# A hashed-attention and gated-MLP kernel: the last output row in three column parts, and one DMA transpose for three head pairs of the last batch

## The chip, the cores and the metric

The kernel runs on one core of one Trainium2 chip. The metric is the device time of one execution in microseconds (us). A core has five engines with a queue each: TensorE (PE; its weight loads are shown as PEld), VectorE (DVE), ScalarE (ACT), GpSimd (POOL) and SyncE (SP), which here only issues DMAs. The median of three runs is the time of a kernel; the profile is a further execution, recorded by the hardware.

## The reference

Four batches, eight heads, 768 positions, 64 columns a head. Queries and keys are hashed to six bits by the signs of a projection; a query attends to the keys with its own hash value only. The result, with heads side by side (3072 rows of 512), goes through a gated layer with a residual.

```python
q_bits = (np.einsum('bhsd,dk->bhsk', q, proj) > 0)          # k likewise; six bits are a bucket
mask = q_bucket[:, :, :, None] == k_bucket[:, :, None, :]
scores = np.where(mask, scale * q @ k.T, -1e9)
attn = softmax(scores);  x = (attn @ v), heads side by side   # 3072 x 512
ffn_out = (gelu(x @ w_gate) * (x @ w_val)) @ w_out            # 512 -> 1536 -> 512
return x + sigmoid(x @ w_res) * ffn_out
```

## The kernel before

**Stages.** The order of all work is written out by hand: each engine runs its instructions in the order in which the code issues them. Heads are taken in pairs, four pairs to a batch, 16 in all. A pair takes nine slots of the main loop (L612 on); in each slot TensorE computes scores for one chunk (`scores`, L380), ScalarE takes their exponential (L385) and TensorE multiplies older exponentials with the values (`values`, L354). At the end of a head, `finish` (L299) divides by the row sums on VectorE and writes the result to `x_tok[b]`, an array of 128 partitions by 4 pairs by 6 blocks by 128 columns, positions on partitions.

**Transposes of x.** The gated layer needs x with its columns on partitions, in `x_sb[b]`. For most pairs `finish` issues a DMA transpose of that pair's six 128x128 blocks on SP's queue (L310). The last pair of a batch goes another way where there is no time for a DMA: `x_turn` (L335) transposes it on TensorE, and ScalarE and VectorE copy it (L340, L341). In the last batch the pairs 0, 1 and 2 go by DMA and pair 3 by `x_turn`.

**The gated layer.** After the last slot of a batch `gv_mm` (L393) and `gate_val` (L403) compute gate and value for twelve blocks of 128 hidden columns, in buffers of the PSUM pool `sc_ps`: TensorE matmuls (L399), ScalarE's Gelu (L416), VectorE's product into `hh` (L419). In the last batch the two first `gv_mm` calls, for pairs 0 to 2, are issued right behind the last attention work (L639), ahead of `x_turn`. `project` (L425) then gives the output, six rows of blocks to a batch, 128 output rows each: four matmuls against `wr` (L431), ScalarE's Tanh (L435), twelve matmuls of `hh` against `wo` into `fps` (L445), two multiply-adds on VectorE (L448, L451), and a store on SP (L453). It is a generator; for batches 0 to 2 its matmuls are spread over the next batch's attention, for the last batch they run at the end, one block row after another. There `fps` lies in `sc_ps` (two buffers, in turn), otherwise in the bank "f" of `mm_ps`, which the last batch's output does not use.

**The last block row.** The very last one (batch 3, t = 5) is computed in two column parts of 384 and 128 columns, `(0, 3)` and `(3, 4)` in units of 128: twelve matmuls, two multiply-adds and a store for the first, then the same for the second.

**DMA lanes.** Each hardware DMA (those issued by SP or ACT, 113 in this kernel) reports its end on one of eight semaphores, here called lanes 0 to 7, taken in turn; SP waits for the lane's previous DMA before it issues a new one on it. At the end of the program, under the line number of the launch (L679), SP waits for everything: first for POOL's DMAs, then lane 0, 1, 2 and so on to lane 7, two semaphores an instruction, then for the engines, and then a barrier over all engines follows. 113 is 14 × 8 + 1, so the last store is on lane 0.

Of the kernel before, what the change touches and what calls it, by code (L numbers as in the profile page):

```python
# [17 lines left out]
def kernel(  # L18
# [12 lines left out]
    nc = tc.nc  # L31
    B, H, S, D = q.shape
# [4 lines left out]
    KM = DMODEL // P  # L37
    KF = DFF // P
    T = S // P
    HP = H // 2  # L40
# [32 lines left out]
    x_tok, x_sb = {}, {}  # L73
# [89 lines left out]
    for s in range(3):  # L163
        n = KF // 3
# [134 lines left out]
    def finish(p, hi):  # L299
        b, hp = divmod(p, HP)  # L300
        if hp == 0 and hi == 0:
            x_tok[b] = x_pool.tile([P, HP, T, 2 * D], BF16, tag="x_tok", name="x_tok")
            x_sb[b] = x_pool.tile([P, HP, T, P], BF16, tag="x_sb", name="x_sb")
        o = av.pop((p, hi))
        rec = sm_pool.tile([P, T], FP32, tag="rec", name="rec")
        nc.vector.reciprocal(rec, o[:, 0:T, D])
        nc.vector.tensor_mul(x_tok[b][:, hp, :, hi * D:(hi + 1) * D], o[:, 0:T, 0:D],
                             rec.unsqueeze(2).to_broadcast([P, T, D]))
        if hi == 1 and (0 < b < B - 1 or hp < HP - (2 if b == 0 else 1)):
            nc.sync.dma_start_transpose(out=x_sb[b][:, hp],  # L310
                                        in_=x_tok[b][:, hp].rearrange("p t n -> p (t n)"))

# [32 lines left out]
    def values(p, c, e):  # L345
        va = vaug[p]
        for i in range(2):
            hi, parts = banks[2 * c + i]
            first = p < HP and (p, hi) not in av
            opened(p, hi)  # L350
            off = i * 512
            for (jt, qt0, nq) in parts:
                for qt in range(qt0, qt0 + nq):
                    nc.tensor.matmul(av[p, hi][:, qt, :], e[:, off:off + P],  # L354
                                     va[:, hi, jt, 0:D + 1],
                                     start=first, stop=(p >= HP and jt == T - 1),
                                     skip_group_check=True)
                    first = False
                    off += P
            if (2 * c + i + 1) % NCH == 0:  # L360
                if p < HP:
                    preset(p, hi)
                if (p, hi) not in late:
                    finish(p, hi)
# [60 lines left out]
    def project(b):  # L425
        hh = hidden[b]
        for t in range(T):
            last = b == B - 1 and t == T - 1
            rps = mm_ps.tile([P, DMODEL], FP32, tag="r", name="rps")
            for kk in range(KM):  # L430
                nc.tensor.matmul(rps, x_sb[b][:, kk, t, :], wr[:, kk, :],  # L431
                                 start=(kk == 0), stop=(kk == KM - 1))
                if kk == KM - 1:
                    th = g_pool.tile([P, DMODEL], FP32, tag="th", name="th")
                    nc.scalar.activation(th, rps, AF.Tanh, scale=0.5)  # L435
                yield
            o = o_pool.tile([P, DMODEL], FP32, tag="o", name="o")
            for k0, k1 in ((0, 3), (3, 4)) if last else ((0, KM),):
                cs = slice(k0 * P, k1 * P)
                if b < B - 1:  # L440
                    fps = mm_ps.tile([P, DMODEL], FP32, tag="f", name="fps")
                else:
                    fps = sc_ps.tile([P, DMODEL], FP32, tag="sp", name="fps")
                for m in range(KF):
                    nc.tensor.matmul(fps[:, cs], hh[:, m, bass.ts(t, P)], wo[:, m, cs],  # L445
                                     start=(m == 0), stop=(m == KF - 1))
                    yield
                nc.vector.scalar_tensor_tensor(o[:, cs], th[:, cs], 1.0, fps[:, cs],  # L448
                                               op0=ALU.add, op1=ALU.mult)
                o3 = o[:, cs].rearrange("p (k n) -> p k n", n=P)  # L450
                nc.vector.scalar_tensor_tensor(o3, o3, 0.5, x_tok[b][:, k0:k1, t, :],  # L451
                                               op0=ALU.mult, op1=ALU.add)
                nc.sync.dma_start(out_t[b, t][:, cs], o[:, cs])  # L453
# [90 lines left out]
    hash_pe((1,), 4, (4,))  # L544
    turns_pe(1, (6, 6, 8, 9))
    at(6, lambda: finish(0, 0), lambda: tr(2, 1))
    at(8, lambda: tr(3, 0))
    at(9, lambda: tr(3, 1))
    at(11, lambda: finish(0, 1))
    at(5, lambda: vals_a(1))  # L550
    at(7, lambda: vals_s(1))
# [60 lines left out]
    for s in range(LAST):  # L612
        p, c = divmod(s, NCH)
        b, slot = divmod(s, NSLOT)
# [10 lines left out]
        if slot == NSLOT - 1:  # L625
            values(*pending.pop(0))
            ps = (HP * (b + 1), HP * (b + 1) + 1)
            if b == 0:
                nc.scalar.activation(table, warm[:, 0:1], AF.Gelu)
                begun = [gv_mm(0, 0, wg, 0, KM - 1)]  # L630
                values(*pending.pop(0))
                begun.append(gv_mm(0, 0, wv, 0, KM - 1))
                x_turn(b, HP - 1)
                hashed(ps, 0, 3)
                gate_val(b, begun, lambda: hashed(ps, 3, 4))
            else:
                mlp_mm(4)
                flush()
                begun = [gv_mm(b, 0, w, 0, KM - 1) for w in (wg, wv)]  # L639
                if b < B - 1:  # L640
                    mlp_mm(NMM)
                    hashed(ps, 0, 2)
                    gate_val(b, begun, lambda: hashed(ps, 2, 4))
                else:
                    x_turn(b, HP - 1)
                    mlp_mm(HELD - 7)
                    gv(b, 0, lambda: mlp_mm(NMM))
                    gate_val(b, begun, lambda: mlp_mm(3))
            done[0] = 0
            mlp.append(project(b))  # L650
# [33 lines left out]
```

## Time and profile before

| what | value |
|---|---|
| median of 3 runs | 347.27 us (346.83 to 347.31) |
| span of the profiled execution | 345.9 us (345.875) |
| TensorE matmul busy | 337.9 us, 98% of the span |
| weight loads busy | 204.4 us, 59% |
| VectorE, ScalarE, GpSimd busy | 191.5, 206.9, 86.1 us |
| granted TensorE clock | full in all 40 slices |
| DMA | 42.90 MB, mean 124 GB/s |
| chain that ended last | TensorE 89%, ScalarE 5%, VectorE 3%, issue 1%, DMA 1% |
| DMA transposes of x | 13, median 2.8 us from issue to landing |
| stores of a whole block row | 23 of 256 KB, median 2.0 us to landing |
| the last two stores | 192 KB and 64 KB, 1.9 and 1.6 us to landing |

The span is that of one recorded execution; the runs' times are measured from outside and lie some 1.4 us above it. Groups are named by line, engine and operation, and `out<-in` by the program's tiles. A chain of waits follows the work that ended last back in time, from each step to what released it. Where a text gives a start to three decimals, it is the start of that instruction in the trace; the views round to one or two.

### The profile page before, as it was taken

The numbers are of one execution on the slowest core, as the hardware profiler recorded it, in microseconds if no ns is written. First come the engines' busy times: TensorE is split into PE (matmuls) and PEld (weight loads), VectorE is DVE, ScalarE is ACT, GpSimd is POOL, SyncE is SP. The second block draws the span as 40 slices with busy tenths as digits, with TensorE's granted clock in tenths as the row PEclk, the third lists the DMA queues.
The fourth block names the chain that finished last, engine by engine and source line by source line (L and its number), as shares of the span: only waits on it lengthen the run. The fifth ranks groups of instructions, "written<-read, shape, count | busy, mean of one in ns | idle before, by whom it ended". The sixth has DMA issues, their size and how long they took to land.

```text
span 345.9 us, 7597 instructions
## 1 busy us (share of the span) xinstructions
PE 337.9 (98%) x3112; PEld 204.4 (59%) x3112; DVE 191.5 (55%) x403; ACT 206.9 (60%) x232; POOL 86.1 (25%) x162
## 2 busy tenths in 40 slices
PE   8999999999999999999999999999999999999994
PEld 5667665655666655555666665655566665556442
DVE  6877757755344856757344784747244444333333
ACT  3889973226999952225999882222999984223120
POOL 4779940343055000270044100242030000000000
PEclk9999999999999999999999999999999999999999
DMA  7939999979376843518366642725430220000022
GB/s 218 377 67 239 247 265 195 159 89 223 121 178 196 195 106 78 106 34 154 85 182 190 223 117 61 136 48 105 79 100 32 55 55 30 32 1 0 32 75 78
DMA packets 71171, 42.90 MB, mean 124 GB/s; under 512 B 49504, under 2 KB 68192, under 8 KB 71136
## 3 DMA queue, kind: packets, MB, share of 16 engines
q1 hardware_dynamic: 64720, 37.17, 42.4%
q0 software_dynamic: 6336, 5.24, 10.2%
q8 instruction: 24, 0.39, 0.4%
q14 instruction: 11, 0.09, 0.1%
q10 hardware_dynamic: 80, 0.00, 0.0%
HBM read 29.36 MB, written 6.29 MB: 103 GB/s over the span
## 4 chain that ended last, share of the span: by engine, by line
PE 89%; ACT 5%; DVE 3%; issue 1%; DMA 1%; SPq 0%; DVEq 0%; ACTq 0%
PE sp L399 36%; PE fps L445 18%; PE sp L380 15%; PE av L354 8%; PE rps L431 5%; ACT e L385 4%; PE hs L205 3%; PE pt L259 2%; DMA ld<-in_q_dram 1%; DVE o L451 1%; DVE o L448 1%; DVE nat L224 0%; PE hs L234 0%; DVE ht L215 0%; DVE hh L419 0%
## 5 line engine op out<-in xcount | busy, mean ns | idle before, releaser
L385 ACT ACTIVATE e<-sp 128x1024 bf16<-128x1024 f32 x144 | 143.8, 1027 | 13.4 <-PE sp L380 7.8
L416 ACT ACTIVATE gt<-sp 128x768 bf16<-128x768 f32 x48 | 38.9, 811 | 93.0 <-PE sp L399 93.0
L380 PE MATMUL sp<-aug,aug 71*128 71x256 bf16 (+1 forms) x384 | 86.1, 325 | 1.1 <-ACT e L385 0.6
L445 PE MATMUL fps<-wo,hh 128*128 128x512 bf16 (+2 forms) x300 | 79.5, 370 | 0.0
L419 DVE TENSOR_TENSOR hh<-gt,sp 128x768 bf16<-128x768 bf16 x48 | 45.8, 955 | 50.5 <-PE sp L399 45.3
L399 PE MATMUL sp<-x_sb,wg 128*128 128x512 bf16 (+1 forms) x384 | 71.0, 326 | 0.1
L399 PE MATMUL sp<-x_sb,wv 128*128 128x512 bf16 (+1 forms) x384 | 70.9, 326 | 0.2 <-DVE hh L419 0.2
L354 PEld LDWEIGHTS <-e 128*128 128x128 bf16 x1152 | 53.3, 97 | 29.1 <-issue 1.4
L354 PE MATMUL av<-va,e 128*128 128x65 bf16 x1152 | 58.9, 193 | 0.1
L399 PEld LDWEIGHTS <-wv 128*128 128x128 bf16 x384 | 37.5, 98 | 25.1 <-issue 0.4
L399 PEld LDWEIGHTS <-wg 128*128 128x128 bf16 x384 | 36.6, 98 | 26.3 <-issue 3.0
L445 PEld LDWEIGHTS <-hh 128*128 128x128 bf16 x300 | 27.5, 97 | 22.7 <-issue 0.3
L448 DVE SCALAR_TENSOR_TENSOR o<-th,fps 128x512 f32<-128x512 f32 (+2 forms) x25 | 16.6, 666 | 36.6 <-PE fps L445 32.0
L380 PEld LDWEIGHTS <-aug 71*128 71x128 bf16 x384 | 29.4, 97 | 10.9 <-issue 2.1
L184 POOL TENSOR_SCALAR nat<-ld 128x768 bf16<-128x768 f32 (+1 forms) x16 | 14.1, 884 | 76.8 <-DMA aug<-nat 73.0
L281 POOL TENSOR_TENSOR v<-ldv 128x384 f32<-128x384 f32 x16 | 16.0, 998 | 66.7 <-DMA ldv<-in_v_dram 66.6
L194 DVE STREAM_TRANSPOSE t<-ld 128x768 f32<-128x768 f32 (+1 forms) x34 | 30.8, 913 | 1.2 <-DMA ld<-in_q_dram 1.0
L333 DVE COPY av<-av 128x390 f32<-128x390 f32 x24 | 13.6, 567 | 30.0 <-PE av L329 30.0
L431 PE MATMUL rps<-wr,x_sb 128*128 128x512 bf16 x96 | 27.1, 378 | 0.0
L435 ACT ACTIVATE th<-rps 128x512 f32<-128x512 f32 x24 | 14.3, 594 | 18.4 <-PE rps L431 18.4
L224 DVE TENSOR_SCALAR nat<-htp 32x72 bf16<-32x72 f32 x96 | 21.9, 228 | 1.8
L451 DVE SCALAR_TENSOR_TENSOR o<-o,x_tok 128x512 f32<-128x512 f32 (+2 forms) x25 | 18.2, 727 | 0.9
(61 smaller groups left out, 191.2 us busy)
## 6 DMA issues: line engine op xcount, KB each, us to landing
ldv<-in_v_dram SPq DMA_DIRECT2D x16, 384.0 KB, 5.5
out_dram<-o SPq DMA_DIRECT2D x23, 256.0 KB, 2.0
ld<-in_q_dram SPq DMA_DIRECT2D x15, 384.0 KB, 5.2
ld<-in_k_dram SPq DMA_DIRECT2D x15, 384.0 KB, 6.2
wg<-in_moe_w_gate_dram POOLq DMA_DIRECT2D x4, 384.0 KB, 8.0
wv<-in_moe_w_val_dram POOLq DMA_DIRECT2D x4, 384.0 KB, 9.8
wo<-in_moe_w_out_dram POOLq DMA_DIRECT2D x3, 512.0 KB, 6.2
wr<-in_moe_w_res_dram POOLq DMA_DIRECT2D x1, 512.0 KB, 12.8
```

Of the source, the lines that this page charges most:

```text
L194: nc.vector.transpose(t32[p, side][:, sl].rearrange("p c h n -> p (c h n)"), raw[p, side][:, sl].rearrange("p c d -> p (c d)"))
L224: engs[a % len(engs)].tensor_scalar(nat_of(x)[32 * a:32 * a + 32, :, D:D + NBITS], ht[32 * j:32 * j + 32, :, NBITS * a:NBITS * (a + 1)], 0 ...
L354: nc.tensor.matmul(av[p, hi][:, qt, :], e[:, off:off + P], va[:, hi, jt, 0:D + 1], start=first, stop=(p >= HP and jt == T - 1), skip_group ...
L380: nc.tensor.matmul(sp[:, off:off + nq * P], ks[0:KA, hi * T + jt, :], qs[0:KA, hi * T + qt0:hi * T + qt0 + nq, :], start=True, stop=True)
L385: nc.scalar.activation(e, sp, AF.Exp, scale=float(ALPHA))
L399: nc.tensor.matmul(sp[:, c0:c1], w[:, kk, bass.ts(m, P)], xs[:, kk, c0:c1], start=(kk == 0), stop=(kk == KM - 1))
L416: nc.scalar.activation(gt, sp[:, 0:S], AF.Gelu)
L419: nc.vector.tensor_mul(hidden[b][:, m, :], gt, ps[1][:, 0:S])
L431: nc.tensor.matmul(rps, x_sb[b][:, kk, t, :], wr[:, kk, :], start=(kk == 0), stop=(kk == KM - 1))
L445: nc.tensor.matmul(fps[:, cs], hh[:, m, bass.ts(t, P)], wo[:, m, cs], start=(m == 0), stop=(m == KF - 1))
L448: nc.vector.scalar_tensor_tensor(o[:, cs], th[:, cs], 1.0, fps[:, cs], op0=ALU.add, op1=ALU.mult)
L451: nc.vector.scalar_tensor_tensor(o3, o3, 0.5, x_tok[b][:, k0:k1, t, :], op0=ALU.mult, op1=ALU.add)
```

## The change

Two edits. In `finish`, the pairs 0, 1 and 2 of the last batch are no longer transposed one by one as they are finished; when pair 2 is finished, a single DMA transpose of eighteen blocks is issued for all three. In `project`, the last block row is computed in three column parts, of 256, 128 and 128 columns. The first two take the two buffers of `sc_ps`, the third takes the bank "f" of `mm_ps`.

```diff
         nc.vector.tensor_mul(x_tok[b][:, hp, :, hi * D:(hi + 1) * D], o[:, 0:T, 0:D],
                              rec.unsqueeze(2).to_broadcast([P, T, D]))
-        if hi == 1 and (0 < b < B - 1 or hp < HP - (2 if b == 0 else 1)):
+        if hi == 1 and b == B - 1:
+            if hp == HP - 2:
+                nc.sync.dma_start_transpose(out=x_sb[b][:, 0:HP - 1].rearrange("p k t n -> p (k t) n"),
+                                            in_=x_tok[b][:, 0:HP - 1].rearrange("p k t n -> p (k t n)"))
+        elif hi == 1 and (b > 0 or hp < HP - 2):
             nc.sync.dma_start_transpose(out=x_sb[b][:, hp],
                                         in_=x_tok[b][:, hp].rearrange("p t n -> p (t n)"))
...
             o = o_pool.tile([P, DMODEL], FP32, tag="o", name="o")
-            for k0, k1 in ((0, 3), (3, 4)) if last else ((0, KM),):
+            for k0, k1 in ((0, 2), (2, 3), (3, 4)) if last else ((0, KM),):
                 cs = slice(k0 * P, k1 * P)
-                if b < B - 1:
+                if b < B - 1 or k0 == KM - 1:
                     fps = mm_ps.tile([P, DMODEL], FP32, tag="f", name="fps")
                 else:
                     fps = sc_ps.tile([P, DMODEL], FP32, tag="sp", name="fps")
```

Two transposes fewer and one store more make 112 hardware DMAs, 14 × 8, so that the last store is on lane 7. The order of the closing waits is the same. No other instruction changes its place on any engine; the first gate matmul of the last batch waits for one DMA where three matmuls waited for one each.

## The prediction

> **What bounds the kernel now.** I read the page's busy table first, then the chain of waits, then the records of the last eight microseconds, because all that the change does to the output lies there.
>
> ```profile
> PE 337.9 (98%) x3112; PEld 204.4 (59%) x3112; DVE 191.5 (55%) x403; ACT 206.9 (60%) x232; POOL 86.1 (25%) x162
> ```
>
> TensorE is busy for 98% of the span, at the full granted clock in every slice. What can be saved without taking work from it is the stretch in which it no longer runs: from its last matmul to the end. The chain of waits over that stretch (start, length, what):
>
> ```profile
> 337.99 0.86 PE rps L431 x4
> 338.85 1.96 PE fps L445 x12
> 340.81 0.04 DVEq L448
> ...
> 340.89 0.56 DVE o L448
> ...
> 341.48 0.56 DVE o L451
> 342.04 0.21 DVE o L448
> ...
> 342.27 0.29 DVE o L451
> ```
>
> The reader is to see that the twelve last 128-column matmuls are not in this chain. VectorE is still at the 384-column part when they end, and the 128-column part queues behind it. The timeline of the same stretch shows it from the other side; the second multiply-add of the last part starts only when the first part's has ended:
>
> ```profile
> 341.48 0.56 DVE L451 SCALAR_TENSOR_TENSOR o<-o,x_tok 128x384 f32<-128x384 f32 x1
> 341.96 0.28 DVE L448 SCALAR_TENSOR_TENSOR o<-th,fps 128x128 f32<-128x128 f32 x1
> 342.06 0.86 SPq L453 DMA_DIRECT2D out_dram<-o  x2
> 342.27 0.29 DVE L451 SCALAR_TENSOR_TENSOR o<-o,x_tok 128x128 f32<-128x128 f32 x1
> ```
>
> After that come a store and SP's closing waits. The view of what SP waited for, the issue table, and the view of the closing line in two stretches (344.1 to 344.6, then 344.6 to 345.2):
>
> ```profile
> SPq L679 <- DMA out_dram<-o: 1.1, 1, 1.1
> ...
> out_dram<-o SPq DMA_DIRECT2D x1, 64.0 KB, 1.6
> ...
> L679 SPq EVENT_SEMAPHORE  x5: 28/28/28, 344.2 to 344.5; - x5
> ...
> L679 SPq EVENT_SEMAPHORE  x3: 28/28/28, 344.8 to 345.0; - x3
> L679 SPq DRAIN  x2: 7/7/7, 345.0 to 345.1; - x2
> ```
>
> The store is issued at 342.589 and has landed at 344.142, 1.553 later. Then SP still works through eight waits, from 344.159 to 344.971, and reaches its first drain at 345.044. They are two per instruction, 0.06 to 0.09 apart, but for one pause of 0.38 between 344.453 and 344.833. All eight stand behind the landing because the last store is hardware DMA number 113 and so counts on lane 0, which is waited for first of the eight lanes. From landing to that drain 0.902 goes by; the rest of the end (to 345.875) is a barrier that the change does not touch.
>
> **The change, part by part.**
>
> *TensorE.* Twelve matmuls of 384 columns become twelve of 256 and twelve of 128; the last twelve of 128 stay. The pitch is 215 ns for 512 columns (four in 0.86) and 163 for 384 (twelve in 1.96), which is 0.41 ns a column and some 2.5 ns besides, so 109 for 256 and 56 for 128. The old 128-column run agrees: its last matmul starts 0.614 after its first, 56 each. Before: 12 × (163 + 56) = 2.63. After: 12 × (109 + 56 + 56) = 2.65. TensorE ends 0.03 later: the last matmul is done and signalled at 341.51 in place of 341.48.
>
> *VectorE.* From 553 and 279 ns for 384 and 128 columns (first multiply-add) a 256-column one takes 416; from 558 and 292 the second takes 425. Part one: its twelve matmuls start at 338.685, the last at 339.886, and with 272 for that one (between 219 and 326) it is signalled at 340.17. The wake-up took 0.08 before, so VectorE starts at 340.25, ends its second step at 341.13, and the store goes out at 341.15. Part two: 341.05 to 341.65 (the next instruction starts 0.08 before the last one ends, as above), store at 341.68. Part three: its matmuls are ready at 341.51 + 0.08 = 341.59, VectorE is free at 341.57. So 341.59 + 0.279 + 0.034 + 0.292 = 342.20, and the store is issued at 342.22. Before it was 342.589: **0.37 earlier**. There is no slack left on either side, 0.02 between the two engines.
>
> *Stores.* One more on SP: 0.332 of issue plus a lane wait, 0.43 in all between two issues. The three go out 0.53 apart, so it lies beside VectorE's work; were VectorE faster it would cost up to 0.43. The last store has the old last one's shape, so it lands 1.55 later, at 343.78. The two old stores were issued 0.52 apart and landed 0.2 apart, thus in parallel.
>
> *The lane.* Two DMAs fewer for x and one more store make 112, so the last store counts on lane 7, whose wait is the last of the eight. The other seven waits are met by landings that lie before 343.25 and run while the last store is under way: SP is free at 342.56, six of them and the pause end by 343.4, lane 6 follows. After 343.78 there remain one wait (0.017) and the step to the drain (0.073): 343.87 in place of 345.04. Of this 1.18 the lane gives 0.902 − 0.09 = **0.81**. Its bounds: 0.81 if all is hidden; 0.43 if the pause of 0.38 falls behind the landing; 0 if a step of this kind only exists while a profile is taken. I take 0.81, since waits already met stand in program order ahead of the one that is not.
>
> *The transposes of x.* Three DMAs of six blocks become one of eighteen, at pair 2. The two early ones (issues of 1.22 at 256.87 and 267.13) go away. Behind each of them on SP stands a store that waits for VectorE until 260.6 and 269.6, so nothing is gained. The one that stays is issued when pair 2's x is written, at 278.55. Its landing has no row: six blocks land in 2.75, twelve (the rows of L248 from 135 us on) in 3.67, so eighteen by the same step in 4.6, at 283.15. The bounds are 3.67 (no worse than twelve) and 3 × 2.75 = 8.3 (one after another). The first matmul that reads it, on the gate weights, starts at 286.00, so there are **7.45 us** of cover; I take 4.6, because the step from six to twelve cost 0.92 and not 2.75. SP is held for 1.22 + 2 × 0.21 = 1.64, at most 3.66; its next store comes at 286.10. TensorE waits for one DMA in place of three and meets it done. If that cover were gone, every microsecond would be TensorE's.
>
> *Sum.* −0.37 − 0.81 + 0 = −1.18 on a span of 345.875, thus 344.70. The median of the runs is 347.27, 1.40 above that span; the difference carried over gives **346.1**.
>
> **The rivals.**
>
> *The pause stays behind the landing* (346.5, chance 0.15). The 0.38 pause follows nothing that it waits for. If it belongs to a place in SP's program rather than to a time, it moves two waits down, because there are two SP instructions fewer ahead of it: to just before lane 7's wait, from 343.25 to 343.66. That is 0.12 ahead of the landing. One place further and it lies open: 347.27 − 1.18 + 0.38 = 346.47. The page "Runtime: NRT & Kernel Launch" of the Trainium skill, section "Instruction fetch mechanics", says that a sequencer is refilled in blocks of 256 instructions, fetched ahead in order and mostly hidden, with a stall for a branch that leaves the window. By that rule the pause should sit behind the branch into the closing block; the trace has none there, and has one six waits later, so the trace does not agree and the cause stays open.
>
> *The waits gain nothing outside the profile* (346.9, chance 0.12). Then only VectorE's 0.37 is left. For it: short steps of a queue are what recording may stretch. Against: the same SP steps of 0.06 to 0.09 stand between issues everywhere.
>
> *The narrow matmuls go at the pace of their weights* (346.6, chance 0.08). A weight load's own row reads 97 ns. If the twelve new 128-column matmuls took 97 in place of 56, TensorE would end 0.49 later, the store would be issued at about 342.71, and −0.81 + 0.12 = −0.69. Against: the old twelve ran at 56 with the same loads, and the 65-column ones of the attention in 0.41 for eight and less.
>
> *Slower: the eighteen-block transpose lands late* (chance 0.05). TensorE stands before the gate matmuls of the last batch until it lands. From 7.45 + 1.18 = 8.6 us on, the kernel is slower than before. At the worst twelve-block landing in the trace (8.29, at 65.2 us, beside weight and input loads), taken 1.5 times, it is 12.4: a stall of 5.0, and 347.27 + 5.0 − 1.2 = 351.1. Against: at 278 us the DMA engines move 30 to 55 GB/s, and even three in a row (8.3) would stall by 0.8 and leave 346.9.
>
> **How the numbers follow.** The forecast has 0.60, the rivals 0.15, 0.12, 0.08 and 0.05. A change under 0.2%, 0.69 us, cannot be told from none here, so faster means below 346.58. Faster: 0.60, 0.12 of the first rival and 0.06 of the third, 0.78. Within: 0.12, 0.03 and 0.02, 0.17. Slower: 0.05. The range goes from 345.7 (the runs of before lie up to 0.44 below their median) to 346.9, which takes in the first three rivals and leaves out the transpose.
>
> **What would show it.** In the changed profile the last store is issued near 342.2 and lands near 343.8; the closing waits for lanes 0 to 5 stand before that landing; the drain follows it within 0.1. The three parts' first multiply-adds start near 340.25, 341.05 and 341.59. The transpose at 278.5 lands below 5 us and TensorE has no idle time at 286. I am wrong if the pause shows behind the landing, if VectorE or TensorE is more than 0.2 late at part three, or if the gate matmuls of the last batch start after 286.1.

## The result

The changed kernel takes 346.02 us (median of four runs, 345.47 to 346.30) against 347.29 for the kernel before; the ratio is 0.9962, 95% interval 0.9950 to 0.9974. The profiled execution spans 344.595 in place of 345.875. Forecast were 346.1 and a span of 344.70.

The times and the span belong to different executions, so one thing about the 1.40 between median and span has to be set right. Each timed run from the changed kernel on has a span and a granted clock of its own on record, and its time lies 1.66 to 1.78 above that span. The profiled execution of the changed kernel is one of its four runs, with 346.30 us, 0.28 above their median. The time of the profiled execution before is not on record; an estimate from its span and 1.71 is 347.6, 0.3 above the median of 347.27.

The chain of waits of the changed kernel, over the last block row (start, length, what):

```profile
337.92 0.86 PE rps L435 x4
338.78 1.32 PE fps L449 x12
340.10 0.04 DVEq L452
...
340.18 0.43 DVE o L452
...
340.64 0.42 DVE o L455
341.06 0.21 DVE o L452
...
341.29 0.29 DVE o L455
341.59 0.21 DVE o L452
...
341.82 0.29 DVE o L455
```

TensorE leaves the chain after the first part's twelve matmuls, at 340.10 in place of 340.81, and VectorE runs the three parts without a gap from there. The third part does not wait for TensorE: its first step starts 0.08 before the second part's last step ends, and the second part's first step starts 0.08 before the first part's last step ends too. Next, the timeline's store line, the issue table, what SP waited for, and the view of the closing line from 342.5 to 343.1 and from 343.1 to 343.8:

```profile
341.09 1.38 SPq L457 DMA_DIRECT2D out_dram<-o  x3
...
out_dram<-o SPq DMA_DIRECT2D x2, 64.0 KB, 1.5
...
SPq L683 <- DMA out_dram<-o: 0.6, 2, 0.4
...
L683 SPq EVENT_SEMAPHORE  x8: 17/28/28, 342.5 to 342.9; - x8
...
L683 SPq EVENT_SEMAPHORE  x2: 28/28/28, 343.2 to 343.7; - x2
L683 SPq DRAIN  x1: 13/13/13, 343.8 to 343.8; - x1
```

Eight closing waits (two for POOL's DMAs, then lanes 0 to 5) have begun by 342.94, seven of them over, while the last store (issued 342.136, landed 343.657) is on its way. The wait for lane 6, at 343.185, follows the landing of the store before it (343.168). Behind the last landing there is one wait, for lane 7 at 343.674, and the drain at 343.757.

Where the 1.28 of the span went, each from the starts in the two traces:

| piece | before | after | difference |
|---|---|---|---|
| span's start to the first matmul into `fps` of the last block row | 338.685 | 338.615 | −0.07 |
| from there to the issue of the last store | 3.904 | 3.521 | −0.38 |
| that store's landing | 1.553 | 1.521 | −0.03 |
| landing to SP's first drain | 0.902 | 0.100 | −0.80 |
| drain to the end | 0.831 | 0.838 | +0.01 |

The first row scatters between executions (338.0 to 339.0 over all the profiles below, without order by kernel), so in what follows a kernel is read from that matmul to the end of its span, here called the tail: 7.19 before, 5.98 after. (The four matmuls against `wr` come ahead of it and do not count; where a text says "the first matmul of the last block row", this one is meant.)

### The profile page after: what moved, and what is told of

It reads as the page before. It is cut to its first block, busy times and chain, and to the rows that moved or that the text cites. A ratio compares the mean times of both kernels' runs of the same rounds, so it can differ in the third digit from the quotient of the medians.

```text
span 344.6 us, 7573 instructions
## 1 busy us (share of the span) xinstructions
PE 335.1 (97%) x3076; PEld 204.8 (59%) x3124; DVE 192.0 (56%) x405; ACT 206.9 (60%) x232; POOL 86.2 (25%) x162
## 4 chain that ended last, share of the span: by engine, by line
PE 88%; ACT 4%; DVE 2%; DMA 2%; issue 2%; SPq 1%; POOL 0%; DVEq 0%; ACTq 0%
PE sp L403 36%; PE fps L449 17%; PE sp L384 15%; PE av L358 8%; PE rps L435 6%; ACT e L389 4%; PE hs L205 3%; DMA ld<-in_k_dram 2%; PE pt L259 1%; DVE o L455 1%; DVE nat L224 0%; SPq L96 0%; DVE o L452 0%; DVE ht L215 0%; PE av L333 0%
## 5 line engine op out<-in xcount | busy, mean ns | idle before, releaser
L449 PE MATMUL fps<-wo,hh 128*128 128x512 bf16 (+2 forms) x286 | 74.7, 361 | 1.6
L403 PE MATMUL sp<-x_sb,wg 128*128 128x256 bf16 (+1 forms) x373 | 70.4, 324 | 0.7
L435 PE MATMUL rps<-wr,x_sb 128*128 128x512 bf16 x90 | 25.3, 378 | 0.2
```

Of the source, the lines that this page charges most:

```text
L403: nc.tensor.matmul(sp[:, c0:c1], w[:, kk, bass.ts(m, P)], xs[:, kk, c0:c1], start=(kk == 0), stop=(kk == KM - 1))
L435: nc.tensor.matmul(rps, x_sb[b][:, kk, t, :], wr[:, kk, :], start=(kk == 0), stop=(kk == KM - 1))
```

## The experiments

The theory is that of the prediction: an earlier last store, and closing waits that run under it, two gains that add. The rivals: the three parts give all of it; the waits cost time only while a profile is taken; the merged transpose has a part of its own.

**The two gains one by one.** Four kernels on one chip: the changed kernel again, and the two parts of the gain crossed. For the lanes the transposes of x in the last batch go in two DMAs, which is one DMA more than in the changed kernel:

```diff
-            if hp == HP - 2:
-                nc.sync.dma_start_transpose(out=x_sb[b][:, 0:HP - 1].rearrange("p k t n -> p (k t) n"),
-                                            in_=x_tok[b][:, 0:HP - 1].rearrange("p k t n -> p (k t n)"))
+            k0, k1 = {1: (0, 2), 2: (2, 3)}.get(hp, (0, 0))
+            if k1:
+                nc.sync.dma_start_transpose(out=x_sb[b][:, k0:k1].rearrange("p k t n -> p (k t) n"),
+                                            in_=x_tok[b][:, k0:k1].rearrange("p k t n -> p (k t n)"))
```

`p3_lane0` is this edit of the changed kernel, `p2_lane7` the same edit of the kernel before. `p3_lane1` is the kernel before with the loop over three parts and the third part's bank "f" alone.

> The changed kernel itself, on the same chip as the next three, as their yardstick. Both theories: a span 1.2 to 1.3 below the kernel before, last store issued 0.37 to 0.45 earlier, 0.10 from the last landing to SP's first drain (0.90 in the kernel before).

> Three parts as in the changed kernel, but the transposes of x in two DMAs (pairs 0 and 1, then pair 2), so 113 hardware DMAs and the last store on lane 0. Theory (two gains that add: an earlier store, and closing waits that run under the last store): the store goes out near 342.2, but 0.5 to 0.9 lie between its landing and the first drain, so the span is about 345.4, 0.4 under the kernel before and 0.8 over the changed one. Rival 1 (the three parts give it all): as fast as the changed kernel. Rival 2 (the closing waits cost only while a profile is taken): the span as in the theory, but the times outside the profile within 0.2 of the changed kernel.

> Two parts as in the kernel before, the transposes of x in two DMAs, so 112 hardware DMAs and the last store on lane 7. Theory: the store goes out near 342.55 as before, 0.10 between its landing and the first drain, a span of about 345.1 and a time 0.8 under the kernel before. Rival 1 (the three parts give it all): the time of the kernel before. Rival 2 (waits cost only in the profile): a span of 345.1 but the time of the kernel before within 0.2.

> The three parts alone, transposes of x as in the kernel before: 114 hardware DMAs, the last store on lane 1. Theory: the store goes out near 342.2; of the eight closing waits one runs before the landing, so 0.45 (no pause) to 0.84 (with it) from the landing to the first drain; span 345.0 to 345.4. If the merged transpose itself brings or costs something, the batch's gate matmuls start at another time than 286.0 here.

| kernel | parts, lane of the last store | first matmul to store | landing to drain | tail against before | ratio to before (95%) |
|---|---|---|---|---|---|
| before | 2, lane 0 | 3.90 | 0.90 | 0 | 1 |
| after_again | 3, lane 7 | 3.52 | 0.10 | −1.20 | 0.9964 (0.9951 to 0.9976) |
| p3_lane0 | 3, lane 0 | 3.52 | 0.90 | −0.40 | 0.9990 (0.9981 to 0.9998) |
| p2_lane7 | 2, lane 7 | 3.90 | 0.27 | −0.61 | 0.9978 (0.9969 to 0.9986) |
| p3_lane1 | 3, lane 1 | 3.52 | 0.82 | −0.48 | 0.9985 (0.9976 to 0.9994) |

In these five the issue of the last store follows the number of parts alone, and the time behind its landing goes with the lane. The ratios over all timed runs say the same: on 347.3 us they are −1.25, −0.35, −0.76 and −0.52, with intervals of 0.3 to 0.4 to either side. So the three parts do not give it all; `p3_lane0` and the changed kernel differ by 0.80 in the tails and by 0.90 in the ratios. The rival that the waits cost time only while a profile is taken stays open: every timed run of these kernels, and not only the profiled one, has a span and a granted clock on record, so none is shown to have run without recording. The closing line of `p3_lane0` from 343.37 to 343.8 and from 343.8 to 344.36, behind a landing at 343.375, is the picture of the kernel before, with three parts:

```profile
L684 SPq EVENT_SEMAPHORE  x5: 27/28/28, 343.4 to 343.7; - x5
...
L684 SPq EVENT_SEMAPHORE  x3: 28/28/28, 344.1 to 344.2; - x3
L684 SPq DRAIN  x2: 7/7/7, 344.3 to 344.3; - x2
```

One line did not come as expected: `p2_lane7` had 0.27 between landing and drain, not 0.10. The view of its closing line from 344.2 to 344.9, where the last store landed at 344.457:

```profile
L684 SPq EVENT_SEMAPHORE  x2: 28/28/28, 344.3 to 344.6; - x2
L684 SPq DRAIN  x2: 7/27/47, 344.7 to 344.8; - x2
```

The wait for lane 6 is at 344.267, that for lane 7 at 344.647, 0.38 later and 0.19 after its landing. This is the pause of the kernel before, two waits further down, where the first rival of the prediction had put it. In `p3_lane1` it stood two waits further up, between lanes 2 and 3 (343.141 and 343.535).

**The pause, the merge and the lanes between.** A DMA more or less shifts both the lane and the place in SP's program. To hold one and move the other, stores of earlier block rows of the last batch are cut, which TensorE's work covers. In thirds, for the rows below 3 or below 4 (for `p3_lane4` in halves, rows 0 to 4):

```diff
-                nc.sync.dma_start(out_t[b, t][:, cs], o[:, cs])
+                if b == B - 1 and t < 3:
+                    for c0, c1 in ((0, 128), (128, 256), (256, DMODEL)):
+                        nc.sync.dma_start(out_t[b, t][:, c0:c1], o[:, c0:c1])
+                else:
+                    nc.sync.dma_start(out_t[b, t][:, cs], o[:, cs])
```

`p3_sep_120` is this on `p3_lane1`, `p2_120` with four rows on `p2_lane7`, `p3_lane4` the halves on the changed kernel; `p2_lane6` is the kernel before with the edit of `finish` alone. `p3_120`, run later, is the changed kernel with four rows in thirds.

> Three parts; the transposes of x one by one as in the kernel before; the stores of block rows 0, 1 and 2 of the last batch cut in three, so 120 hardware DMAs, the last store again on lane 7, and 16 more instructions on SP than in the changed kernel. Theory (earlier store, closing waits under the store; the merged transpose itself brings nothing): 0.10 from the last landing to the first drain, 6.0 from the first matmul of the last block row to the end of the span, the time of the changed kernel within 0.3. If the merged transpose gives part of the gain: slower than the changed kernel by that part. The pause of 0.38 in the closing waits: if it has a fixed place in SP's program (it moved two waits later with two SP instructions fewer, and two earlier with two more), it now falls among the last stores and does not show.

> Two parts, transposes of x in two DMAs, the stores of block rows 0 to 3 of the last batch cut in three: 120 hardware DMAs, last store on lane 7, 16 more SP instructions than p2_lane7. If the pause has a fixed place in SP's program, the 0.27 from landing to drain of p2_lane7 becomes 0.10. If the pause belongs to the time or to the wait for a late lane, 0.27 stays.

> The merged transpose alone, two parts: 111 hardware DMAs, the last store on lane 6, two SP instructions fewer than p2_lane7. Theory: two waits and the step to the drain behind the landing, 0.17, if the pause is not among them. If it has a fixed place, it falls between SP's first and second drain, which are 0.07 apart elsewhere and here about 0.4, so 0.3 more from the first drain to the end.

> The changed kernel with the stores of block rows 0 to 4 of the last batch cut in two: 117 hardware DMAs, the last store on lane 4. Theory: lanes 0 to 3 are waited for under the last store, lanes 4 to 7 behind it: 0.3 from landing to drain, with the pause (fixed place) before them, at the branch behind the last store. Rival (only lane 0 against any other lane counts): 0.10.

> The changed kernel with the stores of block rows 0 to 3 of the last batch cut in three: 120 hardware DMAs, last store on lane 7, eight SP instructions more, so that the pause (fixed place, behind the 207th recorded SP instruction) falls behind the last store, ahead of the closing waits. Theory: 5.98 from the first matmul of the last block row to the end, as in the changed kernel, and its time within 0.3: the extra stores cost nothing and the pause was hidden there too.

| kernel | lane | landing to drain | where the pause stands | tail against before | ratio (95%) |
|---|---|---|---|---|---|
| p3_sep_120 | 7 | 0.08 | ahead of the last store | −0.59 | 0.9984 (0.9975 to 0.9993) |
| p2_120 | 7 | 0.08 | between the first two closing waits | −0.78 | 0.9983 (0.9974 to 0.9991) |
| p2_lane6 | 6 | 0.16 | between the two drains | −0.32 | 0.9992 (0.9982 to 1.0001) |
| p3_lane4 | 4 | 0.27 | between lanes 1 and 2 | −1.03 | 0.9968 (0.9958 to 0.9979) |
| p3_120 | 7 | 0.08 | between the first two closing waits | −1.22 | 0.9966 (0.9954 to 0.9977) |

Counted through the trace, the pause (0.35 to 0.37 between the end of one instruction and the start of the next) stands behind SP's 207th recorded instruction in the kernel before and in every kernel of the two tables but the changed one. There the same place is between the waits for lanes 6 and 7, and it is covered: lane 6's wait ends at 343.213, with 0.352 that makes 343.565, and the last store lands at 343.657. So the pause has a place in the program, not a time; in the changed kernel this is inferred, since its trace can't tell the pause from the wait for the store. In `p2_lane6` it came between the drains, as expected; the closing line from 343.49 to 344.1:

```profile
L683 SPq EVENT_SEMAPHORE  x2: 28/28/28, 343.5 to 343.6; - x2
L683 SPq DRAIN  x2: 7/68/130, 343.6 to 344.0; - x2
```

Each lane behind the last store's costs one more wait (0.10, 0.16, 0.27 for lanes 7, 6, 4), so the rival that only lane 0 is bad falls. With lane 0 the pause comes on top: of the 0.80 between the kernel before and the changed one some 0.3 is the pause and some 0.5 the order of the lanes. That is an estimate, from one step of 0.38 in a row of steps of 0.06 to 0.09; no run has the last store on lane 0 and the pause elsewhere. The ratios do not resolve the pause by itself: hiding it takes 0.17 off the tail of `p2_lane7` (in `p2_120`), while the ratio gets larger by 0.17, within the intervals.

`p3_sep_120` was expected to equal the changed kernel and is slower by 0.6 in the tail, but not through its separate transposes: its gate matmuls start in the range of the others (285.5). The further stores of a row add one instruction each and not two (they need no second wait), so SP has ten recorded instructions more than in the changed kernel and not sixteen (for the same reason `p2_120` has eight more than `p2_lane7`, and in `p3_lane4` the pause came two lanes into the closing waits), and the pause came right ahead of the last store: VectorE was done at 341.67, the store went out at 341.934. And it landed 1.91 after issue, not 1.55: of the 16 engines' reports one came 0.28 after the rest. The DMA view from 342.4 to 343.7 shows what else moved then:

```profile
q1 hardware_dynamic: 144, 0.07, 17.9%
q14 instruction: 1, 0.01, 3.1%
```

One 8 KB packet of the instruction queue, from 342.561 to 343.210, while the store's rows went out; the store's last eight rows start only at 343.207, one after another. That fits an engine held by the packet, but the record does not name the engine of a packet. Such a packet follows the pause in the other traces too, 0.62 to 0.92 behind its end: at 343.69 in `p3_120`, at 345.76 in the kernel before. In the changed kernel it is at 344.214, 0.65 behind the 343.565 inferred above, which supports that place. All this fits a refill of SP's instructions, though no run shows SP waiting for one. The Trainium skill, page "Runtime: NRT & Kernel Launch", section "Instruction fetch mechanics", has instructions refilled in blocks of 256, with a cost at the border that is mostly hidden. A fixed place agrees with a border (207 is what the trace records; what SP runs besides was not counted), and if the pause is such a border, its cost is not hidden in the kernel before, where 0.35 lie open.

The merge's own worth would be what the ratios show beyond the tails. With the separate transposes of `p3_lane1` that is 0.04 (0.52 against 0.48), with the merged one of the changed kernel, taken again, 0.05 (1.25 against 1.20), in intervals of 0.3 to 0.4 to either side: nothing can be seen of it. Over all nine kernels of the two tables, with the transposes in one, two or three DMAs, tail and ratio differ by at most 0.19. The timeline of the changed kernel at the first use of the merged x, and the transpose's line:

```profile
285.70 0.41 PE L358 MATMUL av<-va,e 128*128 128x65 bf16 x8
285.95 1.14 PE L403 MATMUL sp<-x_sb,wg 128*128 128x512 bf16 x6
...
L311 SPq DMA_TRANSPOSE x_sb<-x_tok x1: 2701/2701/2701, 278.5 to 278.5; - x1
```

The gate matmuls follow the attention's with no idle time, 2.9 after the transpose landed (283.09).

**Trying to go further.** The chain says that VectorE's two steps of the last part are next. In three kernels the last part's residual is folded into the accumulation:

```diff
+            if last:
+                g = sm_pool.tile([P, P], FP32, tag="g", name="g")
+                nc.vector.tensor_scalar(g, th[:, DMODEL - P:], 0.5, 0.5, op0=ALU.mult, op1=ALU.add)
+                rg = sm_pool.tile([P, P], FP32, tag="rg", name="rg")
+                nc.vector.reciprocal(rg, g)
+                xg = sm_pool.tile([P, P], BF16, tag="xg", name="xg")
+                nc.vector.tensor_mul(xg, rg, x_tok[b][:, KM - 1, t, :])
...
+                if folded:
+                    nc.tensor.matmul(fps[:, cs], ident, xg[:, gs], start=True, stop=False)
...
+                if folded:
+                    nc.vector.scalar_tensor_tensor(o[:, cs], g[:, gs], 1.0, fps[:, cs],
+                                                   op0=ALU.mult, op1=ALU.mult)
```

> The changed kernel, and in the last 128 columns the residual is folded into the accumulation: x divided by the gate is made on VectorE while it is idle before the last block row and added by one more matmul with the identity, so that one multiply stands at the end in place of two multiply-adds. One matmul more (0.06), one VectorE step less (0.31): the last store goes out 0.25 earlier and lands 0.25 earlier. 112 DMAs, so the pause still stands right before lane 7's wait and ends 0.38 after lane 6's: theory, only about 0.1 of the 0.25 reaches the end, and 0.2 to 0.3 lie between landing and drain. Rival (the pause costs nothing): 0.10 from landing to drain, 0.25 faster than the changed kernel.

> The same with the stores of block rows 0 to 3 cut in three (120 DMAs), which puts the pause ahead of the closing waits. Theory: 0.10 from landing to drain, 5.73 from the first matmul of the last block row to the end, 0.25 faster than the changed kernel.

> The same, with the folded 128 columns in two parts of 64 (four parts, 120 DMAs, last store on lane 7, 32 KB of rows of 256 bytes). The last multiply is 0.07 shorter and the last store lands 0.06 sooner by its size, if 64-column matmuls keep a pitch of about 0.03 as the 65-column ones of the attention do: 5.6 from the first matmul of the last block row to the end. If rows of 256 bytes land slower than rows of 512 bytes, 1.55 or more to landing and no gain over three parts.

All three miss. Ratios to the kernel before: 0.9995 (0.9986 to 1.0003), 0.9987 (0.9978 to 0.9995) and 0.9999 (0.9990 to 1.0008), so each is slower than the changed kernel. The timeline of `fold_120`:

```profile
338.86 0.23 DVE L444 TENSOR_SCALAR g<-th 128x128 f32<-128x128 f32 x1
339.12 0.95 DVE L446 RECIPROCAL rg<-g 128x128 f32<-128x128 f32 x1
...
340.32 0.42 DVE L467 SCALAR_TENSOR_TENSOR o<-th,fps 128x256 f32<-128x256 f32 x1
340.46 0.22 PE L458 MATMUL fps<-xg,ident 128*128 128x128 bf16 x1 [0.28 <-DVE xg L448]
```

The reciprocal takes 0.95 for 128 columns. The preparation does not fit into VectorE's idle time, so part one starts 2.29 after the first matmul and not 1.57, and TensorE waits 0.28 for `xg`. Behind that VectorE does save: from the start of part one to the end of its last step it takes 1.60, in the changed kernel 1.93. But the last store gains only 0.09 of this. VectorE is done at 341.920, but SP is busy with the second store from 341.749 on and gets the third out at 342.187, 0.44 after the second; in the changed kernel the stores are 0.52 apart. So SP's pace of issue is the next limit, which the expectations left out. The pair `fold_112` and `fold_120` differs by the pause again: in `fold_112` it stands between lane 7's wait and the drain (one place later than expected, as SP has one instruction fewer than in the changed kernel), 0.40 from landing to drain against 0.08. With two parts of 64 the stores go out 0.45 and 0.48 apart, as fast as SP issues, while VectorE's steps for them take 0.21 each, so the fourth store waits for SP. Its rows of 256 bytes landed in 1.47, no slower than the 1.55 of 512 bytes. A fold without a reciprocal was not tried; by SP's pace it could bring the last store forward by some 0.09 at most (an estimate, from 0.52 and 0.44 between stores). The changed kernel is the fastest of all, with `p3_120` (0.9966) and `p3_lane4` (0.9968) equal to it within the intervals.

## Why the prediction was right

The mechanism and the sum held: −1.18 forecast, −1.21 measured in the tail, 346.1 against 346.02. That the total came within 0.1 is in part luck: the interval of the measured ratio is 0.4 us to either side, and the 1.40 carried from span to median fitted because both profiled executions lay some 0.3 above their medians (the one before by estimate).

- *TensorE.* A pitch of 109 and 56 ns for 256 and 128 columns was forecast; the trace has 109 and 56, and the 24 narrow matmuls kept it. The rival of weights that set the pace is out.
- *VectorE.* First steps at 340.25, 341.05 and 341.59 were forecast; with the last block row 0.07 earlier in this execution, 340.18, 340.98 and 341.50 are the same but for 0.02 at the third. There the prediction let part three wait for TensorE, by 0.02; in the trace it waits for VectorE. The store went out 0.38 earlier in the tail, 0.37 was forecast.
- *The lane.* −0.81 was forecast, −0.80 measured. `p3_lane0` shows the term by itself: 0.80 in the tail, and 0.90 in the ratios, with some 0.5 to either side. Whether it would be there without any recording no run here shows, so that rival stays open.
- *The pause.* The sum took the pause to be over by 343.4, among the first closing waits; that is not what happened. (In the kernel before it stands behind seven closing waits, counting the two for POOL's DMAs, not six.) The first rival saw that it might have a fixed place and that it would then come just ahead of lane 7's wait, and be covered by 0.12. It has one, and the cover was 0.09. In `p2_lane7`, where lane 6's store is the 192 KB one and lands only 0.2 ahead of lane 7's, 0.19 lies open. So the term of the lane came out right by a margin of 0.09, and that is luck as far as the sum goes.
- *The transpose.* Landing in 4.6 was forecast, 4.55 measured. Mis-sized was SP's hold: 1.64 by the step from six to twelve blocks, 2.70 measured, inside the bound of 3.66. It cost nothing, as SP's next store came at 286.05.

## What to carry to other kernels

When the busiest engine is full, look at what lies between its last instruction and the end: here 3.6 us from there to SP's first drain, made of steps, a store and a row of waits, and 1.2 of it could be had with the same work in other pieces. Cut the last output so that the engine behind never has a large part in hand when the last small one is ready, and no finer than the queue can issue stores. Let the last DMA be the one that is waited for last; the number of DMAs in the whole program decides it, so count again after each edit.

## What the runs showed of the hardware

- In twelve of the fourteen profiles SP pauses for 0.35 to 0.37 us behind its 207th recorded instruction, wherever that falls; in the two of the changed kernel that place lies under the last store. Ahead of the last store the pause delays the store, among closing waits it is free or not, by what is under way.
- SP is held by an x transpose for 1.22, 1.44 and 2.70 us with six, twelve and eighteen blocks: the second step is some six times the first, while the landing grows evenly (2.75, 3.67, 4.55).
- A VectorE reciprocal of 128x128 in 32 bits takes 0.95 us, four times the 0.23 of a scale and add. The Trainium skill, page "VectorE: DVE Perf Modes", section "First, the fixed hardware budget", says that a reciprocal divides iteratively with a repeat count of 8, which agrees in kind.
